# An attention and two MLPs in one kernel: new costs and due times for the planner that orders its instructions

## The chip, the cores and the metric

The kernel runs on one core of a Trainium2 chip. The metric is the device time of one execution in microseconds (us), taken as the median of three runs. The core has five engines that run their own instruction streams: TensorE (PE, matmuls and transposes; its weight loads are shown apart as PEld), VectorE (DVE), ScalarE (ACT), GpSimd (POOL) and SyncE (SP, here only DMA issues). Each stream is in order, so the order in which the program hands instructions to an engine decides what waits behind what.

## The reference

Three stages follow each other, all in fp32, on 12480 tokens of 128 channels. (In the inputs that are used here all weights but two are drawn eight times larger; this changes no shape.)

```python
def mab(q, kv):                        # attention, scale = 1/sqrt(128)
    s = scale * (q @ kv.T); s = s - s.max(-1)
    a = exp(s); a /= a.sum(-1) + 1e-9
    return a @ kv
h = mab(inducing, x)                   # 32 inducing points look at 12480 tokens
x = mab(x, h)                          # 12480 tokens look at 32 points
hid = x @ w_in                         # 128 -> 2048
x = (max(hid, 0) + alpha * min(hid, 0)) @ w_out          # 2048 -> 128
h = x @ w_in2                          # 128 -> 2048
P = a[0] + a[1]*h + a[2]*h**2 + a[3]*h**3
Q = 1 + |b[0]|*|h| + |b[1]|*h**2
out = (P / (Q + 1e-6)) @ w_out2        # 2048 -> 128
```

## The kernel before

A first part, written out by hand (the token list `START` and the code around it), loads x, computes the first attention, prepares the weights and runs the first MLP of the first 480 tokens. It ends about 97 us into the span. What follows is the steady part, in which the change lies.

The steady part goes over NC = 26 chunks of 480 tokens. The 2048 hidden channels are 16 slices of 128. A unit is two slices, so a chunk has NU = 8 units, u = 0 to 7, and there are 208 units k in all. Per chunk and slice, in the kernel's own names:

- First MLP. `la1` is a matmul (L773) into the one bank `h1`. `r` is the ReLU on ScalarE (L778) that empties that bank into SBUF; there are ten SBUF buffers. `lb` is the fp32 matmul back (L786, two records each in the trace) that adds into the one accumulator bank `acc`. After the 16th `lb` one more matmul (L788) adds the linear share, and `x2f` (ScalarE, L802) copies the bank out, `x2h` and `x2l` split the result into two parts.
- Second MLP. `l2` is three fast matmuls per slice (L827 to L829) into one of two double banks `h`. Then per unit: `s` (ScalarE square, L839), `A` (GpSimd, L848), `m` (VectorE, L860), `z` (ScalarE, L844), `q` (VectorE, L873, which frees the `h` bank), `rho` and `r0` (ScalarE, L877 and L882), `ee` and `r1` (VectorE, L892 and L896) and `g` (GpSimd, L907). For u = 7 the last steps are `g0` and `g` on VectorE (L902, L909). Per pair of units there is `B` (GpSimd, L853) and `P` (L864), a DMA issued from GpSimd's queue that adds the tile `b` onto the tile `m` in SBUF; `g` of both units needs it to have landed.
- `o` is the fp32 matmul out (L921, two records each) that adds `g` into the same bank `acc`; after 16 of them `oa` (ScalarE, L933) copies it out, `ot` transposes it on TensorE (L940, again through the bank `h1`), `oy` (L947) copies it and SyncE stores it.
- `at` (L614) transposes the attention weights of a later chunk through `h1` and `as_` (L619) copies them out.

So `acc` changes hands twice per chunk: from the `lb` of one chunk over `x2f` to the `o` of the chunk before, and back over `oa`. `h1` is shared by `la1`, `at` and `ot`.

The order of these instructions is not written by hand. `graph` builds a list of operations, each with its engine, a cost from `COST`, what it must come after, which bank it takes or gives back, and a due time: the unit's nominal start (k times TU = 5.376 us) plus an offset from `DUE`. `arranged` then plays this forward: on each engine it takes the operation that could start first, or one that could start up to `SLACK` later and has an earlier due time. A result is seen on another engine `LAG` after its end, and a bank comes back `LAG` after its reader's end. Only the resulting order goes to the chip. There the engines wait on semaphores, not on planned times.

Of the kernel before, what the change touches and what calls it, by code (L numbers as in the profile page):

```python
# [33 lines left out]


COST = dict(
    la1=0.22, lb=0.81, l2=0.65, o=0.81, mst=0.22, tr=0.51, r=0.46, cp=0.5, s=0.89, z=0.88, rho=0.92, r0=0.9,
    m=1.07, q=1.13, ee=1.07, g0=1.07, r1=1.07, g=1.07, A=1.11, B=2.1, P=0.9, gp=2.22, xl=1.22, cv=0.75,
    sm=(1.04, 0.71, 0.6, 0.55, 0.22), scl=0.45, hi=0.95, lo=2.5, landing=7.0, store=3.0,
)  # L40
LAG = 0.09
TU = 5.376
DUE = dict(
    x2f=3.01, la=1.34, span=1.32, lb1=-1.5, at=-14.51, l2=-9.14, s=-7.21, A=-10.84, m=-29.21, B=-5.93,
    P=-17.7, z=0.92, q=6.15, rho=10.6, r0=9.24, ee=14.43, r1=12.09, g0=15.76, g=14.81, gp=25.78, o=11.51,
    o1=-0.77, ot=6.24, pack=18.22,
)
# [6 lines left out]
def graph(NC, NU, due):  # L54


    ops = {}

    def add(name, eng, cost, after, t, late=0.0, take=None, give=None):
        ops[name] = eng, cost, late, [a for a in after if a in ops or a[0] in LATER], take, give, t  # L60

    C, NUN, CT = COST, NC * NU, NU * TU
    LATER = ("r",)
    add(("x2a", 0), "A", C["cp"], [], 0)
    add(("x2b", 0), "V", 0.66, [("x2a", 0)], 0)
    for i in range(4):
        add(("abs", i), "A", 0.45, [("cv", 4 * i - 8)], 0.5 + 1.2 * i)
        for n in range(max(4 * i - 3, 0), 4 * i + 1):
            add(("cv", n), "V", C["cv"], [("cv", n - 1), ("abs", (n - 1) // 4 if n else -1)], 1.2 * n)
    add(("conv",), "V", 0.0, [("cv", 12)], 1.2 * 13)  # L70
    add(("w2l", 3), "G", 1.25, [], 1)
    for c in range(NC):
        at = c * CT
        x2 = at - due["x2f"]
        if c > 1:
            g, half = c // 4, [("hi", c // 4, 1), ("lo", c // 4, 1)]
            t = x2 - CT - due["at"]
# [24 lines left out]
        for k in range(NU * c, NU * c + NU):
            t, j, odd, dve = k * TU, k // 2, k % 2, k % NU in DVE_G
            for i in range(2):
                add(
                    ("l2", k, i), "P", C["l2"],
                    [("x2l", c), ("x2b", c), ("w2l", 3), ("q", k - 2), ("l2", k, i - 1)], t + due["l2"] + 0.7 * i,
                )
            if c == NC - 1:
                add(("warm", k), "P", 0.5, [("l2", k, 1)], t + due["l2"] + 2.5, take="h1", give="h1")  # L110
            over = [] if odd else [("q", k - 4), ("q", k - 3), ("B", j - 2)]
            add(("s", k), "A", C["s"], [("l2", k, 1)] + over, t + due["s"])
            add(("A", k), "G", C["A"], [("s", k), ("m", k - 2)], t + due["A"])
            add(("m", k), "V", C["m"], [("A", k), ("o", 2 * (j - MBUFS) + 1, 1)], t + due["m"])
            if odd:
                add(("B", j), "G", C["B"], [("s", k), ("P", j - 2)], t + due["B"])
                add(("P", j), "G", C["P"], [("m", k), ("m", k - 1), ("B", j)], t + due["P"], late=C["landing"])
            add(("z", k), "A", C["z"], [("m", k)], t + due["z"])
            add(("q", k), "V", C["q"], [("z", k), ("conv",)] + ([("g", k - ZBUFS)] if k >= ZBUFS else []), t + due["q"])
            add(("rho", k), "A", C["rho"], [("q", k), ("r0", k - 2)], t + due["rho"])  # L120
            bank = [("g" if (k - 1) % NU in DVE_G else "r1", k - 1)]
            add(("r0", k), "A", C["r0"], [("rho", k)] + bank, t + due["r0"])
            add(("ee", k), "V", C["ee"], [("r0", k)], t + due["ee"])
            if dve:
                add(("g0", k), "V", C["g0"], [("ee", k)], t + due["g0"])
                add(("g", k), "V", C["g"], [("g0", k)], t + due["g"])
# [18 lines left out]
def arranged(NC, NU, due=None, span=False):  # L145
    ops = graph(NC, NU, due or DUE)
    names = list(ops)
    at = {n: i for i, n in enumerate(names)}
# [938 lines left out]
```

## Time and profile before

| | before |
|---|---|
| median of 3 runs | 1231.67 us (1231.12 to 1231.79) |
| the profiled execution, its own time | 1232.65 us |
| its span, first to last instruction | 1230.6 us |
| mean granted TensorE clock | 0.993 of full speed |
| busy PE / PEld / DVE / ACT / POOL | 96% / 55% / 84% / 88% / 83% |

The times are those of whole executions; the span lies inside the profiled execution's own time. Durations overlap: an instruction's interval in the trace includes the fill and drain of its pipeline, so the step from one start to the next on a busy engine is often shorter than the interval, and a busy TensorE is not one that loses nothing. On TensorE a sum is therefore made of steps between starts.

### The profile page before, as it was taken

How to read it: one execution, taken by the hardware profiler on the slowest of the kernel's cores; microseconds unless marked ns; L12 is line 12 of the kernel's file. 1: busy time of each engine (PE TensorE's matmuls, PEld its weight loads, DVE VectorE, ACT ScalarE, POOL GpSimd, SP SyncE). 2: the span in 40 equal slices, each digit the busy share in tenths (PEclk: the TensorE clock that was granted, in tenths of full speed). 3: DMA queues.
4: the chain of work that ended last, by engine and by line, in shares of the span. 5: the costliest groups of instructions: out<-in, count | busy, mean ns of one | idle time of the engine just before them, and what ended most of it. 6: DMA issues, size and time to landing. Idle time of an engine off the chain costs nothing.

```text
span 1230.6 us, 12439 instructions
## 1 busy us (share of the span) xinstructions
PE 1176.3 (96%) x4137; PEld 676.0 (55%) x4137; DVE 1032.0 (84%) x1006; ACT 1085.3 (88%) x1485; POOL 1015.6 (83%) x693
## 2 busy tenths in 40 slices
PE   7798999999999999999999999999999999999995
PEld 4444555555555555555555555555555555555552
DVE  3597988888888888888888988888888889888886
ACT  4478989999999999999999999899999999999974
POOL 0126989998899989899988999988999898889886
PEclk9899999999999999999999999999999999999999
DMA  9701454454345545444554544454455445445553
GB/s 231 237 17 32 97 105 99 100 107 93 80 100 105 105 84 117 96 82 95 104 104 89 113 100 88 85 109 100 96 105 104 81 89 112 96 97 105 104 103 74
DMA packets 25260, 124.23 MB, mean 101 GB/s; under 512 B 2428, under 2 KB 6812, under 8 KB 24684
## 3 DMA queue, kind: packets, MB, share of 16 engines
q0 software_dynamic: 14976, 102.24, 41.5%
q1 hardware_dynamic: 10220, 21.20, 6.3%
q8 instruction: 33, 0.54, 0.2%
q14 instruction: 31, 0.25, 0.1%
HBM read 14.80 MB, written 6.39 MB: 17 GB/s over the span
## 4 chain that ended last, share of the span: by engine, by line
PE 72%; POOL 8%; ACT 8%; DVE 6%; issue 4%; DMA 3%; SPq 0%; POOLq 0%; ACTq 0%
PE xa L786 22%; PE oa L921 20%; PE h L773 7%; PE h L827 7%; PE h L829 6%; PE h L828 6%; POOL m L907 3%; ACT h L844 2%; POOL a L848 2%; DMA xs<-in_x_dram 2%; ACT r L778 2%; DVE m L860 2%; POOL b L853 1%; ACT r L882 1%; PE to L940 1%
## 5 line engine op out<-in xcount | busy, mean ns | idle before, releaser
L907 POOL TENSOR_TENSOR m<-m,z 128x960 f32<-128x960 f32 x182 | 449.0, 2481 | 1.5 <-DMA m<-b 1.5
L921 PE MATMUL oa<-m,w2o 128*128 128x480 f32 x832 | 376.1, 572 | 14.3 <-POOL m L907 7.3
L786 PE MATMUL xa<-r,w 128*128 128x480 f32 x832 | 364.4, 568 | 2.6 <-ACT o L933 2.5
L848 POOL TENSOR_SCALAR a<-s,co 128x960 f32<-128x960 f32 x208 | 257.9, 1253 | 72.5 <-ACT s L839 71.9
L892 DVE SCALAR_TENSOR_TENSOR z<-z,r 128x960 f32<-128x960 f32 x208 | 239.2, 1150 | 75.1 <-ACT r L882 74.7
L873 DVE SCALAR_TENSOR_TENSOR z<-s,bab,h 128x960 f32<-128x960 f32 x208 | 251.4, 1211 | 41.9 <-ACT h L844 40.1
L778 ACT ACTIVATE r<-h 128x480 f32<-128x480 f32 x416 | 236.5, 569 | 49.9 <-PE h L773 47.9
L860 DVE TENSOR_TENSOR m<-h,a 128x960 f32<-128x960 f32 x208 | 238.8, 1154 | 28.5 <-POOL a L848 22.7
L921 PEld LDWEIGHTS oa<-m,w2o 128*128 128x128 f32 x832 | 156.2, 191 | 125.2 <-issue 103.3
L786 PEld LDWEIGHTS xa<-r,w 128*128 128x128 f32 x832 | 156.5, 190 | 123.2 <-issue 109.1
L839 ACT ACTIVATE s<-h 128x960 f32<-128x960 f32 x208 | 201.3, 970 | 21.5 <-PE h L829 19.8
L773 PE MATMUL h<-stk,wst 128*128 128x480 f32 x416 | 209.9, 505 | 9.6 <-ACT r L778 8.1
L896 DVE SCALAR_TENSOR_TENSOR z<-z,r 128x960 f32<-128x960 f32 x182 | 209.5, 1151 | 4.3
L877 ACT ACTIVATE rho<-z 128x960 f32<-128x960 f32 x208 | 209.5, 1007 | 2.3 <-DVE z L873 2.2
L853 POOL TENSOR_SCALAR b<-s,co 128x1920 f32<-128x1920 f32 x104 | 211.3, 2032 | 0.0
L882 ACT ACTIVATE r<-rho 128x960 f32<-128x960 f32 x208 | 202.6, 974 | 6.8 <-DVE z L896 5.7
L844 ACT ACTIVATE h<-h 128x960 f32<-128x960 f32 x208 | 200.1, 964 | 7.7 <-DVE m L860 4.1
L827 PE MATMUL h<-xh,w2h 128*128 128x480 f32 x416 | 183.4, 441 | 3.8 <-DVE z L873 3.0
L829 PE MATMUL h<-xl,w2h 128*128 128x480 f32 x416 | 157.9, 380 | 0.0
L828 PE MATMUL h<-xh,w2l 128*128 128x480 f32 x416 | 157.9, 379 | 0.0
L773 PEld LDWEIGHTS h<-stk,wst 128*128 128x128 f32 x416 | 78.0, 188 | 134.6 <-ACT r L778 114.0
L864 POOL DMA_DIRECT2D m<-b x104 | 92.4, 888 | 44.2 <-POOL b L853 26.8
(132 smaller groups left out, 787.5 us busy)
## 6 DMA issues: line engine op xcount, KB each, us to landing
m<-b POOLq DMA_DIRECT2D x104, 960.0 KB, 6.7
xs<-in_x_dram SPq DMA_DIRECT2D x13, 480.0 KB, 14.0
out_dram<-y SPq DMA_DIRECT2D x25, 240.0 KB, 4.2
raw<-in_moe_w_in_dram SPq DMA_DIRECT2D x4, 1024.0 KB, 5.3
raw<-in_moe_w_out_dram SPq DMA_DIRECT2D x4, 1024.0 KB, 12.8
out_dram<-y SPq DMA_DIRECT2D x2, 120.0 KB, 1.9
ind<-in_inducing_dram SPq DMA_DIRECT2D x1, 16.0 KB, 1.8
c<-in_moe_a_dram SPq DMA_DIRECT2D x1, 0.0 KB
```

What stands on the lines that cost most here:

```text
L773: nc.tensor.matmul(t[:, :W], lhsT=wst[:, f * P : (f + 1) * P], rhs=stk[c], start=True, stop=True)
L778: nc.scalar.activation(out=r, in_=h1s.pop((p, i))[:, :W], func=AF.Relu)
L786: nc.tensor.matmul(xacc[c][:, :W], lhsT=w1[:, f, :], rhs=rls.pop((p, i)), start=f == 0, stop=False)
L827: nc.tensor.matmul(t, lhsT=w2h[:, sl], rhs=xh, start=True, stop=False)
L828: nc.tensor.matmul(t, lhsT=w2l[:, sl], rhs=xh, start=False, stop=False)
L829: nc.tensor.matmul(t, lhsT=w2h[:, sl], rhs=xl, start=False, stop=True)
L848: nc.gpsimd.tensor_scalar(out=a, in0=S[k], scalar1=co[:, 3:4], scalar2=co[:, 1:2], op0=ALU.mult, op1=ALU.add)
L860: nc.vector.tensor_tensor(out=Mm[k], in0=hs_[k][:, :, :W], in1=A_.pop(k), op=ALU.mult)
L873: nc.vector.scalar_tensor_tensor(out=Z[k], in0=S.pop(k), scalar=bab[:, 1:2], in1=z, op0=ALU.mult, op1=ALU.add)
L892: nc.vector.scalar_tensor_tensor(out=Z[k], in0=Z[k], scalar=QC, in1=R0[k][:, :, :W], op0=ALU.add, op1=ALU.mult)
L907: nc.gpsimd.tensor_tensor(out=Mm[k], in0=Mm[k], in1=Z.pop(k), op=ALU.mult)
L921: nc.tensor.matmul(oacc[c][:, :W], lhsT=w2o[:, f, :], rhs=(G[k] if i == 0 else G.pop(k))[:, i], start=f == 0, stop=f == NF - 1)
```

## The change

No instruction is added or removed, and no tile, buffer or engine changes. What changes are the numbers with which the planner works, and a few of its rules:

- `COST`: most costs get a third digit and move by one to some per cent. The larger moves: `tr` (a group of four transposes) 0.51 to 0.42, `P` 0.9 to 0.66, `hi` 0.95 to 0.8, `xh` gets a cost of its own (0.57), a landing 7.0 to 6.5, a store 3.0 to 4.0.
- `LAG`: one value of 0.09 becomes one per engine: 0.2 after TensorE, 0.15 after ScalarE, 0.17 after VectorE, 0.14 after GpSimd.
- `STALL`: an operation on TensorE that starts later than the engine was free costs 0.1 more.
- `DUE`: new offsets, and for the steps of a unit eight values, one for each u, in place of one.
- `SLACK` goes from 0.18 to 0.1, and `EARLY` (a limit so wide that it never bound) goes.

```diff
 COST = dict(
-    la1=0.22, lb=0.81, l2=0.65, o=0.81, mst=0.22, tr=0.51, r=0.46, cp=0.5, s=0.89, z=0.88, rho=0.92, r0=0.9,
-    m=1.07, q=1.13, ee=1.07, g0=1.07, r1=1.07, g=1.07, A=1.11, B=2.1, P=0.9, gp=2.22, xl=1.22, cv=0.75,
-    sm=(1.04, 0.71, 0.6, 0.55, 0.22), scl=0.45, hi=0.95, lo=2.5, landing=7.0, store=3.0,
+    la1=0.217, lb=0.804, l2=0.651, o=0.804, mst=0.2, tr=0.42, r=0.455, cp=0.47, xh=0.57, s=0.865, z=0.855, rho=0.9,
+    r0=0.89, m=1.07, q=1.127, ee=1.072, g0=1.072, r1=1.072, g=1.072, A=1.118, B=2.15, P=0.66, gp=2.26, xl=1.174, cv=0.75,
+    sm=(1.04, 0.71, 0.6, 0.55, 0.22), scl=0.45, hi=0.8, lo=2.56, landing=6.5, store=4.0,
 )
-LAG = 0.09
+LAG = dict(P=0.2, A=0.15, V=0.17, G=0.14, S=0.0)
+STALL = 0.1
 DUE = dict(
-    x2f=3.01, la=1.34, span=1.32, lb1=-1.5, at=-14.51, l2=-9.14, s=-7.21, A=-10.84, m=-29.21, B=-5.93,
-    P=-17.7, z=0.92, q=6.15, rho=10.6, r0=9.24, ee=14.43, r1=12.09, g0=15.76, g=14.81, gp=25.78, o=11.51,
-    o1=-0.77, ot=6.24, pack=18.22,
+    x2f=-0.45, la=-9.06, span=2.97, lb1=-13.61, at=-97.53, o=-23.76, o1=-13.46, ot=22.31, pack=12.69,
+    l2=(29.67, 35.58, -79.83, -40.1, -11.09, -27.3, -24.5, -43.29),
+    s=(-17.84, -32.0, -16.83, -26.56, -59.46, -97.25, -31.04, -54.94),
+    A=(-63.73, -120.71, -103.15, -88.14, -48.47, -71.46, -128.35, -89.09),
...
+    B=(-54.95, -120.41, -105.91, -26.76, 36.86, -21.45, -83.45, 36.32),
+    P=(187.3, 56.68, 20.63, 25.06, 67.81, -5.11, 38.88, -25.19),
...
+    gp=(89.99, 44.35, 54.18, 117.38, 95.33, 178.76, 75.12, 95.23),
 )
-EARLY, SLACK = 9007.5, 0.18
+SLACK = 0.1
...
-            add(("x2h", c), "A", C["cp"], [("x2f", c), ("l2", NU * (c - 2) + NU - 1, 1)], x2 + 0.6)
+            add(("x2h", c), "A", C["xh"], [("x2f", c), ("l2", NU * (c - 2) + NU - 1, 1)], x2 + 0.6)
...
-            t, j, odd, dve = k * TU, k // 2, k % 2, k % NU in DVE_G
+            t, j, odd, u = k * TU, k // 2, k % 2, k % NU
...
-            add(("s", k), "A", C["s"], [("l2", k, 1)] + over, t + due["s"])
+            add(("s", k), "A", C["s"], [("l2", k, 1)] + over, t + due["s"][u])
...
-                s = max(free[e], ready[i], bank[take[i]], when[i] - EARLY)
+                s = max(free[e], ready[i], bank[take[i]])
...
-        free[e] = t = s + cost[i]
+        free[e] = t = s + cost[i] + (STALL if e == "P" and s > free[e] + 1e-9 else 0.0)
...
-            bank[give[i]] = t + LAG
+            bank[give[i]] = t + LAG[e]
...
-            ready[n] = max(ready[n], t + late[i] + (LAG if eng[n] != e or late[i] else 0.0))
+            ready[n] = max(ready[n], t + late[i] + (LAG[e] if eng[n] != e or late[i] else 0.0))
```

The other steps of a unit (`m`, `z`, `q`, `rho`, `r0`, `ee`, `g0`, `g`, `r1`) get their eight values and their `[u]` in the same way. P and B exist for odd u alone.

## Rows read from the trace of the kernel before

**Rows 1.** the page, costliest groups: us busy, mean ns of one

```profile
L786 PE MATMUL xa<-r,w 128*128 128x480 f32 x832 | 364.4, 568 | 2.6 <-ACT o L933 2.5
```

**Rows 2.** table by stretch: length; busy PE, PEld, DVE, ACT, POOL; clock; DMA; GB/s

```profile
96.80:132.38 35.58, 29.59 (x87) 15.80 (x86) 27.28 (x31) 30.16 (x43) 23.71 (x19) 0.95 0.27 55
132.38:183.71 51.33, 47.73 (x152) 27.25 (x150) 46.40 (x43) 46.91 (x63) 46.20 (x30) 0.97 0.50 102
656.61:699.34 42.73, 42.36 (x139) 24.40 (x138) 37.02 (x34) 39.69 (x54) 36.98 (x25) 1.00 0.48 99
699.34:742.74 43.40, 42.52 (x139) 24.38 (x138) 37.21 (x36) 40.66 (x56) 39.43 (x28) 1.00 0.47 97
183.71:1171.24 987.53, 976.73 (x3153) 560.41 (x3152) 853.52 (x772) 918.95 (x1232) 882.49 (x596) 1.00 0.48 98
1171.24:1230.60 59.36, 45.39 (x139) 25.05 (x137) 46.47 (x43) 36.62 (x42) 44.85 (x29) 0.96 0.45 92
```

**Rows 3.** timeline of TensorE, two stretches (start, us, engine, line)

```profile
609.30 4.99 PE L786 MATMUL xa<-r,w 128*128 128x480 f32 x12
...
656.61 0.75 PE L788 MATMUL xa<-stk,mst 128*128 128x480 f32 x1
657.20 0.57 PE L614 MATMUL ta<-ident,a 120*128 120x120 f32 x4
658.06 2.65 PE L921 MATMUL oa<-m,w2o 128*128 128x480 f32 x6 [0.28 <-issue]
...
661.59 0.49 PE L773 MATMUL h<-stk,wst 128*128 128x480 f32 x1
661.92 0.38 PE L827 MATMUL h<-xh,w2h 128*128 128x480 f32 x1
...
662.35 0.38 PE L829 MATMUL h<-xl,w2h 128*128 128x480 f32 x1
662.74 0.49 PE L773 MATMUL h<-stk,wst 128*128 128x480 f32 x1
...
664.36 0.38 PE L773 MATMUL h<-stk,wst 128*128 128x480 f32 x1
...
667.08 0.49 PE L773 MATMUL h<-stk,wst 128*128 128x480 f32 x1
...
668.23 0.49 PE L773 MATMUL h<-stk,wst 128*128 128x480 f32 x1
...
669.58 0.48 PE L773 MATMUL h<-stk,wst 128*128 128x480 f32 x1
```

**Rows 4.** timeline of ScalarE in the same stretch

```profile
662.12 0.57 ACT L778 ACTIVATE r<-h 128x480 f32<-128x480 f32 x1 [0.58 <-PE h L773]
662.59 0.97 ACT L882 ACTIVATE r<-rho 128x960 f32<-128x960 f32 x1
```

**Rows 5.** waits of the weight loads, 183.71 to 1171.24 us: total, times, longest

```profile
PEld h L773 <- ACT r L778: 93.9, 183, 0.8
...
PEld h L827 <- DVE z L873: 9.7, 33, 0.4
```

**Rows 6.** timeline of TensorE where the accumulator changes hands the other way

```profile
721.13 0.75 PE L773 MATMUL h<-stk,wst 128*128 128x480 f32 x1
722.41 1.07 PE L786 MATMUL xa<-r,w 128*128 128x480 f32 x2 [0.53 <-ACT o L933]
```

**Rows 7.** timeline of GpSimd at the end of a chunk

```profile
654.62 2.16 POOL L853 TENSOR_SCALAR b<-s,co 128x1920 f32<-128x1920 f32 x1
657.09 0.88 POOL L864 DMA_DIRECT2D m<-b  x1 [0.30 <-POOL b L853]
...
665.05 1.14 POOL L848 TENSOR_SCALAR a<-s,co 128x960 f32<-128x960 f32 x1 [1.45 <-ACT s L839]
```

**Rows 8.** timeline of VectorE, first reader of that DMA's result

```profile
664.66 1.16 DVE L902 TENSOR_TENSOR r<-m,r 128x960 f32<-128x960 f32 x1
```

**Rows 9.** the page, DMA issues (KB each, us from issue to landing)

```profile
m<-b POOLq DMA_DIRECT2D x104, 960.0 KB, 6.7
```

More of the change, by code (lines that the diff above doesn't have):

```diff
@@ L36 @@
 COST = dict(
-    la1=0.22, lb=0.81, l2=0.65, o=0.81, mst=0.22, tr=0.51, r=0.46, cp=0.5, s=0.89, z=0.88, rho=0.92, r0=0.9,
-    m=1.07, q=1.13, ee=1.07, g0=1.07, r1=1.07, g=1.07, A=1.11, B=2.1, P=0.9, gp=2.22, xl=1.22, cv=0.75,
-    sm=(1.04, 0.71, 0.6, 0.55, 0.22), scl=0.45, hi=0.95, lo=2.5, landing=7.0, store=3.0,
-)
-LAG = 0.09
+    la1=0.217, lb=0.804, l2=0.651, o=0.804, mst=0.2, tr=0.42, r=0.455, cp=0.47, xh=0.57, s=0.865, z=0.855, rho=0.9,
+    r0=0.89, m=1.07, q=1.127, ee=1.072, g0=1.072, r1=1.072, g=1.072, A=1.118, B=2.15, P=0.66, gp=2.26, xl=1.174, cv=0.75,
+    sm=(1.04, 0.71, 0.6, 0.55, 0.22), scl=0.45, hi=0.8, lo=2.56, landing=6.5, store=4.0,
+)
+LAG = dict(P=0.2, A=0.15, V=0.17, G=0.14, S=0.0)
+STALL = 0.1
 TU = 5.376
 DUE = dict(
-    x2f=3.01, la=1.34, span=1.32, lb1=-1.5, at=-14.51, l2=-9.14, s=-7.21, A=-10.84, m=-29.21, B=-5.93,
-    P=-17.7, z=0.92, q=6.15, rho=10.6, r0=9.24, ee=14.43, r1=12.09, g0=15.76, g=14.81, gp=25.78, o=11.51,
-    o1=-0.77, ot=6.24, pack=18.22,
+    x2f=-0.45, la=-9.06, span=2.97, lb1=-13.61, at=-97.53, o=-23.76, o1=-13.46, ot=22.31, pack=12.69,
+    l2=(29.67, 35.58, -79.83, -40.1, -11.09, -27.3, -24.5, -43.29),
+    s=(-17.84, -32.0, -16.83, -26.56, -59.46, -97.25, -31.04, -54.94),
+    A=(-63.73, -120.71, -103.15, -88.14, -48.47, -71.46, -128.35, -89.09),
+    m=(-108.75, -22.15, -116.09, -46.72, -47.13, -42.75, -50.15, -148.19),
+    B=(-54.95, -120.41, -105.91, -26.76, 36.86, -21.45, -83.45, 36.32),
+    P=(187.3, 56.68, 20.63, 25.06, 67.81, -5.11, 38.88, -25.19),
+    z=(-26.7, -63.52, -31.2, -26.94, 5.39, 24.47, 11.89, 15.71),
+    q=(32.02, 39.1, 47.63, 65.87, 13.6, 133.96, 50.31, 70.75),
+    rho=(36.83, 86.45, 150.83, 117.66, 71.04, 81.94, 112.77, 38.48),
+    r0=(78.33, 29.52, 26.2, -49.91, 50.51, 19.63, -30.96, -28.81),
+    ee=(62.9, 108.52, 89.98, 43.06, 77.86, 74.23, 43.3, 78.62),
+    g0=(70.57, 75.02, 1.99, 84.61, 105.19, 73.56, 80.62, 149.83),
+    g=(58.94, 3.2, 116.11, 8.69, 83.04, 10.67, 31.27, 107.91),
+    r1=(40.2, 67.74, 21.19, 94.45, -8.56, 116.72, 111.67, -32.38),
+    gp=(89.99, 44.35, 54.18, 117.38, 95.33, 178.76, 75.12, 95.23),
 )
-EARLY, SLACK = 9007.5, 0.18
+SLACK = 0.1
 DVE_G = (7,)
@@ L106, in graph @@
                     ("l2", k, i), "P", C["l2"],
-                    [("x2l", c), ("x2b", c), ("w2l", 3), ("q", k - 2), ("l2", k, i - 1)], t + due["l2"] + 0.7 * i,
+                    [("x2l", c), ("x2b", c), ("w2l", 3), ("q", k - 2), ("l2", k, i - 1)], t + due["l2"][u] + 0.7 * i,
                 )
             if c == NC - 1:
-                add(("warm", k), "P", 0.5, [("l2", k, 1)], t + due["l2"] + 2.5, take="h1", give="h1")
+                add(("warm", k), "P", 0.5, [("l2", k, 1)], t + due["l2"][u] + 2.5, take="h1", give="h1")
@@ L111, in graph @@
             over = [] if odd else [("q", k - 4), ("q", k - 3), ("B", j - 2)]
-            add(("s", k), "A", C["s"], [("l2", k, 1)] + over, t + due["s"])
-            add(("A", k), "G", C["A"], [("s", k), ("m", k - 2)], t + due["A"])
-            add(("m", k), "V", C["m"], [("A", k), ("o", 2 * (j - MBUFS) + 1, 1)], t + due["m"])
+            add(("s", k), "A", C["s"], [("l2", k, 1)] + over, t + due["s"][u])
+            add(("A", k), "G", C["A"], [("s", k), ("m", k - 2)], t + due["A"][u])
+            add(("m", k), "V", C["m"], [("A", k), ("o", 2 * (j - MBUFS) + 1, 1)], t + due["m"][u])
@@ L115, in graph @@
             if odd:
[L116 to L120, printed above, removed]
-            bank = [("g" if (k - 1) % NU in DVE_G else "r1", k - 1)]
@@ L122, in graph @@
[L122 to L126, printed above, removed]
-            else:
-                add(("r1", k), "V", C["r1"], [("ee", k)], t + due["r1"])
-                add(("g", k), "G", C["gp"], [("r1", k)], t + due["gp"])
+                add(("B", j), "G", C["B"], [("s", k), ("P", j - 2)], t + due["B"][u])
@@ new lines, in graph @@
+                add(("P", j), "G", C["P"], [("m", k), ("m", k - 1), ("B", j)], t + due["P"][u], late=C["landing"])
+            add(("z", k), "A", C["z"], [("m", k)], t + due["z"][u])
+            add(("q", k), "V", C["q"], [("z", k), ("conv",)] + ([("g", k - ZBUFS)] if k >= ZBUFS else []), t + due["q"][u])
+            add(("rho", k), "A", C["rho"], [("q", k), ("r0", k - 2)], t + due["rho"][u])
+            bank = [("g" if (k - 1) % NU in DVE_G else "r1", k - 1)]
+            add(("r0", k), "A", C["r0"], [("rho", k)] + bank, t + due["r0"][u])
@@ L130, in graph @@
+            add(("ee", k), "V", C["ee"], [("r0", k)], t + due["ee"][u])
+            if u in DVE_G:
+                add(("g0", k), "V", C["g0"], [("ee", k)], t + due["g0"][u])
+                add(("g", k), "V", C["g"], [("g0", k)], t + due["g"][u])
+            else:
+                add(("r1", k), "V", C["r1"], [("ee", k)], t + due["r1"][u])
+                add(("g", k), "G", C["gp"], [("r1", k)], t + due["gp"][u])
             if odd:
-                for u in (k - 1, k):
-                    ops["g0" if ("g0", u) in ops else "g", u][3].append(("P", j))
+                for n in (k - 1, k):
+                    ops["g0" if ("g0", n) in ops else "g", n][3].append(("P", j))
```

## The prediction, made before the change was run

> **What bounds the kernel now.** I read the table by stretch first. The steady part, 183.71 to 1171.24 us, is 23 chunks and takes 987.53 us, 42.94 us a chunk; single chunks take 42.73 to 43.40 [rows 2]. TensorE shows 976.73 us busy there. That looks full, but its intervals overlap, so I counted the work of a chunk by steps between starts. The step inside a run of `lb` or `o` records is 0.402 us: twelve records last 4.99, of which the last alone is 0.568, and 4.42 / 11 = 0.402 [rows 1, 3]. The step of an `l2` matmul is 0.217: 661.92 to 662.35 is two steps, 0.43 [rows 3]. A `la1` into which the engine flows takes the same step. A chunk has 64 records of 0.402 (25.73), 48 `l2` steps, 16 `la1` and one closing matmul (65 x 0.217 = 14.11), and eight transposes of about 0.10 (0.84): 40.7 us. So TensorE loses 42.94 - 40.7 = 2.2 us a chunk, 52 us in the steady part. ScalarE with 918.95 / 23 = 39.95 and GpSimd with 38.4 us busy a chunk lie just under it [rows 2]. TensorE is the bound, with little room beneath it.
>
> Then the timeline of TensorE at the start of a chunk, for where the 2.2 us go [rows 3]. The reader is to see two kinds of hole.
>
> First, `la1`. The one at 664.36 has an interval of 0.38; those at 661.59, 662.74, 667.08, 668.23 and 669.58 have 0.48 or 0.49, about 0.11 more: their weight load waited for the ReLU to empty the bank `h1`. With one slice of `l2` between two of them, 661.59 to 662.74 is 1.15 where 0.217 + 0.651 = 0.868 is work: 0.28 lost. With one `o` between, 667.08 to 668.23 is 1.15 against 0.217 + 0.804 = 1.02: 0.13. The next, 1.35, loses 0.33. With 0.11 for the first and for the one at 667.08 that is 0.96 us in this chunk. Over 23 chunks: 6.4 us behind one `l2` slice and 15.7 behind one `o` or `lb`. The chain of waits over the stretch agrees in kind: 183 weight loads of `la1`, eight a chunk, waited for the ReLU, whereas only 33 of `l2` waited for `q` [rows 5].
>
> Second, the accumulator. From the transposes at 657.20 (0.42 of work) to the first `o` at 658.06 there are 0.44 us lost while `x2f` empties `acc` [rows 3]; 23 times, 10.1 us. On the way back, at 722.41, `lb` finds TensorE idle for 0.53 us [rows 6]; I saw it in the chunks of 43.40 us, at most every fourth, about 3 us in all.
>
> Outside the steady part TensorE is idle for 35.58 - 29.59 and 51.33 - 47.73, together 9.6 us, in the first two chunks and 59.36 - 45.39 = 14.0 us in the last stretch [rows 2].
>
> **The change, part by part.** No instruction is added or taken away, so every gain and loss is a wait that the new order has or lacks.
>
> *The bank `h1`.* Under the old numbers a `la1` is thought to be possible 0.09 + 0.46 + 0.09 = 0.64 after the last, which fits behind one `l2` slice (0.65). The new ones say 0.2 + 0.455 + 0.15 = 0.805. The trace sides with the new: a ReLU behind which ScalarE flows on takes 0.47 from start to start [rows 4], and behind one slice 0.28 is lost. With 0.805 the bank is 0.154 late behind a slice, more than the new `SLACK` of 0.1, so the planner puts something else there. I take all 6.4 us of that. Behind one `o` or `lb` (0.804) it is late by 0.001, within `SLACK`, and `la1` is due earlier than most of those, so the rule of choice still takes it and pays `STALL`; only where the offsets arrange it otherwise does the hole go. I take 4 of 15.7 us; the ends are 0 and 15.7.
>
> About this hole the Trainium skill has a rule: TensorE's queue can pull a weight load ahead of matmuls in flight (page "TensorE: Matmul & The Clock Gate", section "Architectural detail: the array is 16× 32×32, not 1× 128×128"). By it the 0.11 would be hidden and only the 0.154 would be worth anything; the trace disagrees for a load that itself waits for a semaphore, which shows 0.11 more each time [rows 3].
>
> *The accumulator.* The old numbers see 0.09 + 0.5 + 0.09 against 0.51 of transposes, 0.17 of waiting; the new 0.2 + 0.47 + 0.15 - 0.42 = 0.40. What could fill it is `l2`, if it is not yet done, or a second transpose, which shares `h1`. I expect little: 1 of 10.1 us, ends 0 and 10.1. On the way back 1 of 3, ends 0 and 3.
>
> *First chunks and tail.* 23.6 us of idle time, set by the latency through four engines. The offsets differ by u only and not by chunk, so they are not made for these ends. I take a gain of 3, with -5 and +8 as ends.
>
> *P and GpSimd.* Before, `P` is due 17.7 before its unit, ahead of `A` (10.84 before). Now `P` of u = 7 is due 25.19 before its unit, but `A` of the next unit 63.73 - 5.38 = 58.35 before that same point: whenever both are ready, `A` goes first (1.12 by its new cost, 1.14 in the trace [rows 7]), and in places a `B` with it, whose step to the next start is 657.09 - 654.62 = 2.47 [rows 7]. `P` then goes out up to 3.6 us later. It lands 6.7 us after its issue [rows 9]; the one of 657.09 is first read at 664.66, 7.57 later, so the cover is 0.87 us [rows 7, 8]. Beyond it `g0` waits on VectorE, with the `m` of the next unit queued behind it, and `g` waits on GpSimd with the next `A` behind it. I take a loss of 3 us over the run, with 0 and 20 as ends (rival D).
>
> *Sum.* 6.4 + 4 + 1 + 1 + 3 - 3 = 12.4 us. The profiled execution's own time is 1232.65, which gives 1220.3; the median lies 0.98 below that execution, so 1219.3: **1219 us**.
>
> **Rivals.**
>
> A, *smaller gain: the held weight load is no loss*. If TensorE would have spent the 0.11 anyway, only 0.154 x 23 = 3.5 of the `la1` holes can go: 3.5 + 0 + 1 + 1 + 3 - 3 = 5.5, 1226 us. For it: the skill's rule above. Against it: the steps of 1.15 in [rows 3].
>
> B, *larger gain*. All 22 us at `h1`, half of the 10.1 at `acc` and 1 on the way back, with no loss on GpSimd: 28, so 1203.6 us. For it: the new numbers see these holes at nearly their measured size. Against it: the choice is greedy, and at `acc` little is at hand.
>
> C, *no change*. TensorE's holes close and the time appears as waits for `g` or `q`, because the loop through ScalarE, GpSimd and VectorE sets the pace, or because the order comes out nearly the same: 1231.7 us. For it: ScalarE at 39.95 of 42.94. Against it: 33 waits for `q` of 9.7 us in 23 chunks [rows 5], and ScalarE's steps are shorter than its intervals (0.47 for 0.57 [rows 4]).
>
> D, *slower, through `P` on GpSimd*. If `P` of u = 7 goes behind one `A` and one `B` in each chunk, it is 3.6 - 0.87 = 2.7 us late. GpSimd idles 42.94 - 38.4 = 4.5 us a chunk [rows 2] and takes up part; if 0.8 us a chunk is left over, 25 chunks lose 20 us. The gains of the sum, 15.4, come to half at most while TensorE waits for `g`: 20 - 7.7 = 12 us slower, 1244 us. It decides as soon as `P` of units 6 and 7 stands more than 0.87 us later against its first reader, so that DMA waits of `g` and `g0` appear in every chunk. For it: the cover is short and the due times allow it. Against it: the planner makes `g` wait for a landing of 6.5, so it can see this loss.
>
> **How the numbers follow.** A measurement of this kernel can tell about 0.2% (2.5 us) from no change. The forecast has 0.52, with its own range 1206 to 1229, from the ends of its terms; A 0.08; B 0.12; C 0.10; D 0.18. Faster is forecast, A and B: 0.72. Same is C: 0.10. Slower is D: 0.18. The range goes down to B's 1203 and up to 1240, which leaves half of B and over half of D out, 0.16.
>
> **What would show it.** Right: in the steady part fewer than the 183 waits of `la1` for the ReLU, none behind a single `l2` slice, a chunk of 42.2 to 42.6 us, and the hole before the first `o` still there. Wrong: the same count of waits with a shorter chunk (then the gain lies elsewhere), waits of `g` and `g0` for the DMA in each chunk (D), more waits of `l2` for `q` (C), or a change that lies in the first 184 or last 60 us.

## The result and the profile after

The changed kernel takes 1215.89 us in the median of four runs (1215.13 to 1218.17), the kernel before 1231.73 us in four runs on the same chip. The ratio is 0.9875 with a 95% interval of 0.9858 to 0.9892: 15.8 us less, and the interval lies clear of 1. The profiled execution has a span of 1214.3 us, 16.3 less than before.

The table by stretch of the changed kernel, with the columns of [rows 2] and cut at the same events (where the `lb` chains of chunks 0, 1, 2 and 25 end, with their closing matmul; the two single chunks in the middle are rows 3 and 4):

```profile
95.85:131.22 35.37, 30.03 (x88) 16.57 (x86) 25.46 (x29) 28.41 (x41) 22.12 (x18) 0.90 0.28 56
131.22:182.15 50.93, 45.60 (x151) 26.65 (x150) 45.82 (x43) 46.77 (x62) 47.20 (x32) 1.00 0.50 102
646.95:688.45 41.50, 41.10 (x139) 24.83 (x138) 36.97 (x35) 39.09 (x54) 37.17 (x25) 1.00 0.50 101
688.45:732.05 43.60, 42.00 (x140) 24.81 (x138) 37.49 (x36) 39.77 (x56) 39.90 (x27) 1.00 0.48 96
182.15:1152.71 970.56, 953.94 (x3153) 569.82 (x3152) 857.51 (x773) 907.71 (x1232) 883.62 (x596) 1.00 0.49 100
1152.71:1214.30 61.59, 47.72 (x139) 25.91 (x137) 48.91 (x46) 38.56 (x45) 46.26 (x29) 0.92 0.43 88
```

The reader is to see where the time went. The steady part of 23 chunks fell from 987.53 to 970.56 us, by 17.0, or 0.74 a chunk. The two first chunks together fell by 0.6 us, the last stretch grew by 2.2. And the chunks are less alike than before: they come in a cycle of four, and the last two of it take about 41.5 us (before: about 42.8), the second 42.2 (before: 42.9), the first 43.60 (before: 43.40).

The timeline of TensorE at the start of a good chunk, against [rows 3] (`la1` is L787, `l2` L841 to L843, `o` L935, the closing matmul L802, `at` L628):

```profile
646.95 0.76 PE L802 MATMUL xa<-stk,mst 128*128 128x480 f32 x1
647.54 0.57 PE L628 MATMUL ta<-ident,a 120*128 120x120 f32 x4
648.52 2.65 PE L935 MATMUL oa<-m,w2o 128*128 128x480 f32 x6 [0.40 <-POOL b L867]
...
651.88 0.38 PE L841 MATMUL h<-xh,w2h 128*128 128x480 f32 x1
...
652.53 0.38 PE L787 MATMUL h<-stk,wst 128*128 128x480 f32 x1
652.75 0.38 PE L841 MATMUL h<-xh,w2h 128*128 128x480 f32 x1
...
658.15 0.75 PE L787 MATMUL h<-stk,wst 128*128 128x480 f32 x1
658.74 1.77 PE L935 MATMUL oa<-m,w2o 128*128 128x480 f32 x4
...
661.64 0.38 PE L787 MATMUL h<-stk,wst 128*128 128x480 f32 x1
...
663.17 0.38 PE L787 MATMUL h<-stk,wst 128*128 128x480 f32 x1
663.39 1.77 PE L935 MATMUL oa<-m,w2o 128*128 128x480 f32 x4
664.88 0.50 PE L787 MATMUL h<-stk,wst 128*128 128x480 f32 x1
```

The reader is to see two things. First, between one `la1` and the next there are now mostly two `o` (four records), two `lb`, two slices of `l2`, or a mix of them; those at 652.53, 661.64 and 663.17 have the interval 0.38 of one that TensorE flows into. The ones at 658.15 and 664.88 show 0.75 and 0.50, but they begin while the `o` before them still stream (663.39 + 4 x 0.402 = 665.00) and lose nothing: the interval alone does not tell, the step does. Second, the hole at the accumulator is still there, 0.40 us idle before 648.52, longer than the 0.28 of before. The view puts it down to `b` on GpSimd, which ended last; the `g` that this `o` reads were done long before, and what it waits for is `x2f`, which empties the bank just then:

```profile
647.85 0.57 ACT L816 COPY xf<-xa 128x480 f32<-128x480 f32 x1
```

To have the whole steady part and not one chunk, I went over all TensorE records of it and added up by how much each ends later than its work (0.402 or 0.217 us, the steps of the prediction) after the end of the one before it. The sums, sorted by what came too late, in us over the 23 chunks:

| kernel | `la1` held | `l2` late | first `o` or `lb` after `acc` changes hands, and other late `o`, `lb` | steady part |
|---|---|---|---|---|
| before | 23.1 | 10.0 | 15.8 | 987.5 |
| after | 8.5 | 7.1 | 17.6 | 970.6 |
| e1_old_offsets | 13.8 | 10.6 | 28.5 | 991.8 |
| e2_old_numbers | 33.2 | 16.5 | 26.0 | 1014.9 |
| e3_la1_earlier | 64.9 | 2.8 | 18.0 | 1024.7 |
| e4_h1_later | 4.5 | 33.1 | 27.1 | 1001.9 |
| s_old | 24.6 | 7.7 | 15.8 | 987.2 |
| s_new | 11.9 | 10.5 | 26.3 | 986.5 |
| s_lag | 14.4 | 10.3 | 22.2 | 985.4 |
| s_cst | 29.9 | 11.3 | 18.7 | 997.4 |
| s_fix | 6.3 | 2.3 | 15.3 | 962.8 |
| e7_no_scale | 4.0 | 4.4 | 17.7 | 963.5 |

From before to after 14.6 us go at `la1` and 2.9 at `l2`; small waits before `ot`, which the table leaves out, give 0.9, and the accumulator costs 1.8 more. That is 16.6 of the 17.0 us.

### The profile page after: what moved, and what is told of

Same layout as the page of the kernel before. It is cut to its first block, busy times and chain, and to the rows that moved or that the text cites. A ratio compares the mean times of both kernels' runs of the same rounds, so it can differ in the third digit from the quotient of the medians.

```text
span 1214.3 us, 12431 instructions
## 1 busy us (share of the span) xinstructions
PE 1154.3 (95%) x4137; PEld 686.4 (57%) x4137; DVE 1035.9 (85%) x1006; ACT 1074.2 (88%) x1485; POOL 1017.5 (84%) x693
## 3 DMA queue, kind: packets, MB, share of 16 engines
q0 software_dynamic: 14976, 102.24, 42.2%
## 4 chain that ended last, share of the span: by engine, by line
PE 60%; POOL 15%; DVE 10%; ACT 8%; issue 3%; DMA 3%; SPq 0%; POOLq 0%; ACTq 0%
PE oa L935 19%; PE xa L800 16%; POOL m L921 6%; PE h L787 6%; PE h L841 5%; PE h L843 5%; PE h L842 5%; POOL a L862 4%; POOL b L867 4%; DVE m L874 3%; DMA xs<-in_x_dram 2%; DVE z L887 2%; ACT s L853 2%; DVE z L906 2%; ACT r L896 2%
## 5 line engine op out<-in xcount | busy, mean ns | idle before, releaser
L921 POOL TENSOR_TENSOR m<-m,z 128x960 f32<-128x960 f32 x182 | 430.3, 2463 | 36.8 <-DVE z L910 35.4
L935 PE MATMUL oa<-m,w2o 128*128 128x480 f32 x832 | 373.2, 572 | 16.1 <-POOL b L867 7.6
L800 PE MATMUL xa<-r,w 128*128 128x480 f32 x832 | 376.1, 570 | 3.3 <-ACT o L947 2.8
L862 POOL TENSOR_SCALAR a<-s,co 128x960 f32<-128x960 f32 x208 | 248.8, 1217 | 36.8 <-ACT s L853 34.9
L874 DVE TENSOR_TENSOR m<-h,a 128x960 f32<-128x960 f32 x208 | 235.8, 1154 | 39.5 <-POOL a L862 38.9
L887 DVE SCALAR_TENSOR_TENSOR z<-s,bab,h 128x960 f32<-128x960 f32 x208 | 247.2, 1209 | 2.3 <-ACT h L858 1.5
L787 PE MATMUL h<-stk,wst 128*128 128x480 f32 x416 | 236.8, 570 | 10.5 <-ACT r L792 10.4
L935 PEld LDWEIGHTS oa<-m,w2o 128*128 128x128 f32 x832 | 156.1, 191 | 140.0 <-issue 109.7
L800 PEld LDWEIGHTS xa<-r,w 128*128 128x128 f32 x832 | 155.3, 190 | 107.3 <-issue 87.8
L853 ACT ACTIVATE s<-h 128x960 f32<-128x960 f32 x208 | 197.0, 971 | 20.8 <-PE h L843 18.4
L858 ACT ACTIVATE h<-h 128x960 f32<-128x960 f32 x208 | 199.6, 964 | 13.6 <-DVE m L874 11.8
L867 POOL TENSOR_SCALAR b<-s,co 128x1920 f32<-128x1920 f32 x104 | 205.4, 1975 | 0.0
L841 PE MATMUL h<-xh,w2h 128*128 128x480 f32 x416 | 186.9, 449 | 6.6 <-DVE z L887 6.2
L843 PE MATMUL h<-xl,w2h 128*128 128x480 f32 x416 | 157.9, 379 | 0.0
L787 PEld LDWEIGHTS h<-stk,wst 128*128 128x128 f32 x416 | 78.4, 189 | 115.6 <-ACT r L792 92.9
L878 POOL DMA_DIRECT2D m<-b x104 | 92.4, 888 | 33.2 <-POOL b L867 30.6
## 6 DMA issues: line engine op xcount, KB each, us to landing
xs<-in_x_dram SPq DMA_DIRECT2D x13, 480.0 KB, 13.9
raw<-in_moe_w_out_dram SPq DMA_DIRECT2D x4, 1024.0 KB, 11.9
```

Source lines behind the costliest of these rows:

```text
L787: nc.tensor.matmul(t[:, :W], lhsT=wst[:, f * P : (f + 1) * P], rhs=stk[c], start=True, stop=True)
L800: nc.tensor.matmul(xacc[c][:, :W], lhsT=w1[:, f, :], rhs=rls.pop((p, i)), start=f == 0, stop=False)
L841: nc.tensor.matmul(t, lhsT=w2h[:, sl], rhs=xh, start=True, stop=False)
L862: nc.gpsimd.tensor_scalar(out=a, in0=S[k], scalar1=co[:, 3:4], scalar2=co[:, 1:2], op0=ALU.mult, op1=ALU.add)
L867: nc.gpsimd.tensor_scalar(out=b, in0=SP.pop(j), scalar1=co[:, 2:3], scalar2=co[:, 0:1], op0=ALU.mult, op1=ALU.add)
L874: nc.vector.tensor_tensor(out=Mm[k], in0=hs_[k][:, :, :W], in1=A_.pop(k), op=ALU.mult)
```

## The experiments

A word on what the theories of the later runs rest on. The planner's play-forward can also be used the other way: keep an order as it is and play it with other numbers. With the changed kernel's numbers the order of the kernel before ends 21.1 us after that of the changed kernel, though its own plan, made with the old numbers, ended 5.0 us before the changed kernel's. These are ends on paper, and no times of the chip; only their differences are used, and the runs are the test of them. (Code cuts below are shortened.)

**Half of the change at a time.** e1 has the new numbers and the old offsets:

```diff
 COST, LAG, STALL, SLACK: as changed
-    l2=(29.67, 35.58, -79.83, ...), s=(-17.84, ...), ...
+    x2f=3.01, la=1.34, ..., l2=-9.14, s=-7.21, ...        # as before, the same for every u
```

> The changed kernel's costs, lags, stall and slack with the single offsets of the kernel before. In this order 47 la1 stand behind one o, 14 behind one lb and none behind one l2 slice (before: 84, 19 and 25). Theory T (the gain is TensorE no longer held at the bank h1, whatever offsets bring it about): 42 x 0.13 + 25 x 0.28 = 12.5 us less than before, about 1219. Rival R (the gain comes from the eight offsets per step, the new numbers by themselves do nothing): about 1231.

Measured: 1239.15 us, ratio 1.006 (1.004 to 1.0081). Both theories miss. The holds of `la1` did fall, from 23.1 to 13.8 us, but the first `o` and `lb` on a changed accumulator lost 28.5 in place of 15.8.

e2 is the other half:

```diff
 DUE: as changed
-COST = dict(la1=0.217, ...); LAG = dict(P=0.2, A=0.15, V=0.17, G=0.14, S=0.0); STALL = 0.1; SLACK = 0.1
+COST = dict(la1=0.22, ...);  LAG = dict.fromkeys("PAVGS", 0.09);               STALL = 0.0; SLACK = 0.18
+            over = [("s", k - 1)] if odd else [...]       # and m after the m of its pair
```

> The kernel before's costs, lag, slack and no stall with the changed kernel's eight offsets per step (and two added precedences that keep the halves of a pair in order). In this order 101 la1 stand behind one o, 27 behind one lb, 26 behind one l2 slice. Theory T: those holds cost as before, 1231 or more (before had 128 of them, this has 154: up to 1235). Rival R: the offsets alone bring the gain, about 1216 to 1220.

Measured: 1266.8 us, ratio 1.0281 (1.026 to 1.0302). Rival R falls: the eight offsets by themselves bring no gain, they lose 34.8 us. Theory T has the direction, but only 10 of the 27 us more in the steady part are holds of `la1`; the rest is `l2` and the accumulator. So each half alone is slower than before, and the two together are faster.

**The holds of `la1` alone.** e3 moves only `la1`, only on TensorE:

```diff
+        if run[n][0] == "la1" and run[n - 2][0] == run[n - 1][0] in ("o", "lb") and run[n - 3][0] == "la1":
+            run[n - 1], run[n] = run[n], run[n - 1]
```

> The changed kernel with the order of TensorE alone altered: 109 more la1 stand behind one o or lb, each moved ahead of one of the two that it stood behind; all other engines keep their order. Theory T: 109 x 0.12 = 13 us more than the changed kernel, about 1229. Rival A of the prediction (a held weight load is no loss, or TensorE makes it up): no change, 1216.

Measured: 1271.12 us, ratio 1.0323 (1.0298 to 1.0347), 55 us more than the changed kernel. A held `la1` is a loss, so the rival of this run falls, but the price was far off: 56.4 us more of holds, 0.5 us for each of the 109 and not 0.12. The timeline says why. TensorE and then ScalarE, at one such place (`la1` is L800, `lb` L813, `s` L866, `r` L805):

```profile
701.60 0.38 PE L800 MATMUL h<-stk,wst 128*128 128x480 f32 x1
701.82 0.96 PE L813 MATMUL xa<-r,w 128*128 128x480 f32 x2
703.28 0.48 PE L800 MATMUL h<-stk,wst 128*128 128x480 f32 x1 [0.50 <-ACT r L805]
```

```profile
701.80 0.97 ACT L866 ACTIVATE s<-h 128x960 f32<-128x960 f32 x1
702.67 0.56 ACT L805 ACTIVATE r<-h 128x480 f32<-128x480 f32 x1
```

The `la1` of 701.60 is done soon, but ScalarE's next instruction in its order is `s`, and `r` comes after it, at 702.67. So the bank is free only at 703.2, and TensorE stood idle 0.50 us. In the steady part 127 `la1` now stand behind one `o` or `lb`, and lose 64.9 us. 69 of them have `s` in front of their `r` in this way, and lose 53 us; 40 lose the 0.12 that was expected. An order is one thing over all engines, and a move on one of them alone meets the places of the others.

e4 gives the old planner one better number:

```diff
-            bank[give[i]] = t + LAG
+            bank[give[i]] = t + LAG + (0.35 if give[i] == "h1" else 0.0)
```

> The kernel before with one number altered: the planner counts the bank h1 as free 0.35 us later than it did (0.99 us after la1 in place of 0.64). In this order 18 la1 stand behind one o, 14 behind one lb, none behind one l2 slice. Theory T: 66 x 0.13 + 5 x 0.13 + 25 x 0.28 = 16 us less than before, about 1216. Rival R: the old offsets keep the old pace, about 1231.

Measured: 1247.8 us, ratio 1.0129 (1.0104 to 1.0154). The holds fell to 4.5 us, more than in the changed kernel, and the time rose all the same: `l2` was late by 33.1 us in place of 10.0. In the list of waits its weight loads wait longer for `q`, the reader that frees their bank (before, 9.7 us in 33 [rows 5]):

```profile
PEld h L827 <- DVE z L873: 24.5, 38, 1.2
```

This is rival C's mechanism, the loop over `q`, in a kernel whose order was not made for it, and the accumulator cost 11.3 us more besides. Theory T in its simple form (remove the holds and the time follows) is thereby out. What the chip pays is all waits together.

**Is it the numbers or the freedom of the offsets?** That is theory F against rival S, as the two expectations below put them. For s_old and s_new I searched offsets for each u anew, with the same start, the same random steps and the same count, once with the old numbers and once with the new:

```diff
 s_old:  COST, LAG = 0.09, no STALL, SLACK = 0.18 as before;  DUE searched (8 per step)
 s_new:  COST, LAG per engine, STALL, SLACK = 0.1 as changed;  DUE searched (8 per step)
 both, and s_lag, s_cst, s_fix below: s and m of a pair in order, as in e2
```

(With the changed kernel's own offsets this addition leaves the order as it is.)

> Offsets for each u, searched anew by 400,000 random steps that shorten the planner's own end, with the kernel before's costs, lag and slack and no stall, starting from the single offsets of the kernel before. Its plan ends 0.8 us before the plan of the kernel before and 13.6 us before that of s_new. Theory F (the chip follows the new numbers, so a plan made with the old ones slips): played forward with the new numbers this order ends 1.0 us later than before's, so about 1232, and later than s_new. Rival S (the freedom of eight offsets and the search make the gain): clearly faster than before, 1216 to 1225, and if the old plan held, faster than s_new.

Measured: 1234.2 us, ratio 1.0008 (0.9995 to 1.0021). As theory F says: a plan that is shorter on paper than before's is not faster on the chip.

> The same search, the same start and the same number of steps, but with the changed kernel's costs, lags, stall and slack. Theory F: its plan ends 13.2 us before the order of the kernel before played with the same numbers, and 7.8 us after the changed kernel's, so about 1218 to 1224. Rival S: no faster than s_old.

Measured: 1229.61 us, ratio 0.9972 (0.9961 to 0.9984). Faster than s_old by 4.6 us, with a plan that is 13.6 us longer: rival S is not borne out. The size is missed: 1218 to 1224 was expected. The holds of `la1` halved, but the accumulator cost 26.3 us. My search also ended 7.8 us short of the changed kernel's offsets on paper; on the chip it is 13.7.

Then each half of the new numbers with the same search:

```diff
 s_lag:  LAG per engine as changed;  COST, SLACK, no STALL as before;  DUE searched
 s_cst:  COST, STALL, SLACK as changed;  LAG = 0.09 as before;  DUE searched
```

> As s_old, but of the changed kernel's numbers the planner has the lags alone (0.2, 0.15, 0.17, 0.14 in place of 0.09); costs, slack and the missing stall are the kernel before's; the same search, start and number of steps. Theory L (of the new numbers the lags carry the gain): played with all new numbers this order ends 9.9 us before s_old's, so 1222 to 1230, faster than before. Rival (costs and stall carry it): as s_old, 1232 or more.

> The other half: the changed kernel's costs, stall and slack with the old lag of 0.09 on every engine; the same search. Theory L: its plan promises a pace that the chip does not hold; played with all new numbers it ends 4.7 us after s_old's, so 1235 to 1242. Rival: the costs and the stall are enough, 1216 to 1228.

Measured: s_lag 1228.52 us, ratio 0.9976 (0.9961 to 0.9991); s_cst 1238.8 us, ratio 1.0051 (1.0031 to 1.007). In these searches it is the lags that matter. In the orders made with 0.09 (e4 with its extra 0.35 aside) `la1` is held 23 to 33 us on the chip, in those made with the new lags 6 to 14 (e3, which was altered afterwards, aside). But each set of numbers was searched once. The changed kernel's offsets, with the same numbers as s_new, are 13.7 us faster than s_new, so what a search happens to find weighs more than the 5 to 10 us between these four runs. That the lags carry the gain is supported by them and not shown.

**`P` on GpSimd (rival D).** e5 moves `P` of units 6 and 7 in the kernel before, e6 every `P` in the changed one, in both behind the next operation of GpSimd:

```diff
+        if ops[n][0] == "P":                         # e5: only u = 6, 7; not where the next one is a g that reads it
+            ops.insert(next_of_pool(n), ops.pop(n))
```

> The kernel before with the 26 P of units 6 and 7 moved behind the next operation of GpSimd (a g, 2.2 us); all other orders unchanged. Their cover before the first reader was 0.8 to 1.5 us, so they land about 1.3 us too late. Theory D of the prediction (a P that loses its cover sets the pace): 0.8 to 1.35 us a chunk, 20 to 34 us more, 1252 to 1266. Rival: GpSimd's and VectorE's idle time takes it up, 1232 to 1236.

Measured: 1236.41 us, ratio 1.0032 (1.0017 to 1.0047). The wait is there, in the list of waits of this run (24 times, `g0` for the DMA; before, 1.0 us in 3):

```profile
DVE r L913 <- DMA m<-b: 18.1, 24, 1.9
```

But the steady part grew by 1.5 us only, the last stretch by 3.7. The rest of the waits cost nothing on TensorE in the steady part. The price of D, 0.8 us a chunk, was about twelve times too high for the 0.75 us that a landing was late here on average; 2.7 us, as D had it, was not tried.

> The changed kernel with all 104 P moved behind the next operation of GpSimd (mostly a g of 2.2 us or x2l of 1.2). In its trace a P starts 10.0 to 13.9 us before its first reader, 3.3 us or more beyond the landing of 6.7. If only the cover counts: 1216, no change. If a later P costs by itself (the DMA's traffic meets other work, or g behind it comes too early and holds GpSimd): 1220 or more.

Measured: 1230.3 us, 14.4 more than the changed kernel, so the first bound falls. The steady part lost 4.4 us, the first two chunks 6.8 and the last stretch 2.9. GpSimd's waits for the DMA, 1.5 us or less in either kernel, came to 2.7 us in the steady part, 5.9 before it and 4.8 behind it: the covers that I read were those of the steady part, and at the ends, where nothing fills TensorE, they were shorter. How much of the 4.4 us is landing and how much the changed order of `g` I did not separate.

**All waits together.** No single wait gave the times of these runs, but the play-forward has them. With the changed kernel's numbers the orders of e1, e2, e3, e4 and e6 end 20.8, 53.7, 59.4, 37.5 and 13.3 us after the changed kernel's, and those of s_old, s_new, s_lag and s_cst 22.1, 7.8, 12.2 and 26.8; measured were 23.3, 50.9, 55.2, 31.9 and 14.4, and 18.3, 13.7, 12.6 and 22.9. Only e5 is far off, 17.0 us over the kernel before where 4 to 5 were measured, and there the landing is the reason: `P` with 0.66, 6.5 and a lag of 0.14 lands 7.3 us after its start in the plan and 6.7 in the trace [rows 9], and with a landing of 5.9 the play-forward gives 4.4.

**Where the changed plan slips.** I set the planner's own start of each operation against the start in the trace. In the kernel before the operations fall behind their plan by 1.3 us over one chunk (`g` at 657.73 by 0.0, `g` at 703.87 by 1.3), a little at every hold. In the changed kernel it is 0.3 us over a chunk, until one place in every fourth chunk. GpSimd there (`g` L921, the scaling of the attention weights L595, `A` L862):

```profile
692.08 2.52 POOL L921 TENSOR_TENSOR m<-m,z 128x960 f32<-128x960 f32 x1
695.02 1.05 POOL L595 TENSOR_TENSOR att<-att,mm 120x512 f32<-120x512 f32 x1 [0.41 <-DVE mm L594]
696.03 2.23 POOL L921 TENSOR_TENSOR m<-m,z 128x960 f32<-128x960 f32 x1
698.25 1.14 POOL L862 TENSOR_SCALAR a<-s,co 128x960 f32<-128x960 f32 x1
```

The scaling waits 0.41 us for two VectorE instructions that the planner doesn't know, and takes 1.0 us to the next start where `COST` says 0.45. The `g` at 696.03 and what follows it on GpSimd are 1.2 to 1.4 us further behind the plan than what came before. e7 leaves the scaling out:

```diff
     def a_scale(g):
-        ...; nc.vector.tensor_scalar(...); nc.vector.reciprocal(...); nc.gpsimd.tensor_tensor(...)
+        SUM.pop(g)
```

> The changed kernel in its own order, without the scaling of the attention weights of the later chunks (two VectorE instructions and one on GpSimd, six times; the weights stay unnormalised). In the changed kernel's trace the operations behind it start 1.2 to 1.4 us later than planned from there on. Theory F: the six chunks of 43.6 us lose about 1.3 us each, 8 us in all, 1208. Rival: those chunks are long because of the hi and lo parts, 1215 to 1217.

Measured: 1207.82 us, ratio 0.9798 (0.9779 to 0.9817), 8 us less, and the chunk in question in the table by stretch:

```profile
516.39:558.73 42.34, 41.48 (x140) 24.89 (x138) 36.51 (x34) 39.55 (x56) 38.87 (x26) 1.00 0.49 99
```

42.34 us against 43.60. The other three kinds of chunk are as they were. That is the time that theory F gave. The hi and lo parts, which e7 still has, are not what these 1.3 us were; but e7 takes away work as well as a wrong number, and does not tell the two apart.

s_fix does the full work and tells the planner of it:

```diff
-    ..., scl=0.45, hi=0.8, lo=2.56, landing=6.5, store=4.0,
+    ..., scd=0.47, scl=1.03, hi=0.68, lo=1.45, landing=6.5, store=4.0,
...
-                add(("scl", g), "G", C["scl"] * n, [("sm", g, 4), ("at", c - 1)], tg - 2)
+                add(("scd", g), "V", C["scd"], [("sm", g, 4), ("scl", g - 1)], tg - 3)
+                add(("scl", g), "G", C["scl"] * n, [("scd", g), ("at", c - 1)], tg - 2)
...
+ DUE: searched again from the changed kernel's offsets
```

> The changed kernel's numbers with four of them set to what its trace shows: the scaling of the attention weights (scl) 1.03 in place of 0.45 with its two VectorE instructions as an operation of their own (0.47), lo 1.45 in place of 2.56, hi 0.68 in place of 0.8; then the same search from the changed kernel's offsets. Theory F: played with these numbers its plan ends 12.4 us before the changed kernel's order, so about 1204. Rival: what is left is latency that no number holds, 1213 to 1219.

Measured: 1206.44 us, ratio 0.9789 (0.9769 to 0.9808). It is faster than both kernels, by 9.5 us than the changed one, where 12 were expected. Its steady part in the table by stretch, and the chunk that was 43.60:

```profile
180.06:1142.84 962.78, 952.09 (x3153) 568.47 (x3152) 853.68 (x770) 904.96 (x1231) 880.82 (x596) 1.00 0.49 101
682.62:724.13 41.51, 41.08 (x139) 24.91 (x138) 37.18 (x35) 40.23 (x57) 40.16 (x28) 1.00 0.44 89
```

41.86 us a chunk, 1.2 above the counted work of 40.7, and over half of that is the accumulator. The gain lies where the changed plan slipped: of the cycle of four chunks the first is 2.1 us shorter, and the others, but for three single ones, are within 0.2 us of what they were. What the four numbers did is not separated on the chip, one from the other or from the further search. On paper the scaling is the smaller part: with `scl` put back and `scd` taken out the changed kernel's order ends 4.6 us earlier and this one at the same point, whereas with `lo` put back to 2.56 this one ends 11.1 us later.

## Why the prediction was right

The forecast was 1219 us, 12.4 us of gain; measured were 15.8, within its own range of 1206 to 1229. That range is not what the ends of the terms add up to (18.6 us slower to 43.2 faster), so to land in it took some luck: the mechanism at `la1` was right, and the errors of the other terms nearly cancelled. By its steps:

- *What bounds the kernel.* TensorE, with 2.2 us lost a chunk: right. The losses that went are TensorE's, and in this change the time followed them.
- *`la1` behind one `l2` slice*, 6.4 us: right. After the change no `la1` of the steady part stands there; with the new lags its bank would be late by 0.154, more than `SLACK`.
- *`la1` behind one `o` or `lb`*, 4 of 15.7: mis-sized. About 8 went in the balance (14.6 of 23.1 in all, less the 6.4). Of the loss behind one `o` or `lb` itself nearly all went: 96 `la1` stood there in the steady part and lost 15.8 us, 22 stand there now and lose 3.1. The other `la1` lose 5 us where they lost 1, 3.5 of it in five of the chunks in which the plan slips. I held that the rule of choice would still take a bank that is late by 0.001. It would, but the offsets arrange it otherwise: two units go through their `l2` together, and two `o` stand between `la1`. The witness that I named failed as well: 186 loads wait for the ReLU, where 183 did. By my own list the same count with a shorter chunk was to mean that the gain lies elsewhere; it does not, and it was the sign that was badly chosen. The chunk of 42.2 to 42.6 us came out at 42.20 on average, with single ones from 41.5 to 43.6.

The list of waits of the weight loads in the changed kernel, against [rows 5]:

```profile
PEld h L787 <- ACT r L792: 76.9, 186, 1.5
...
PEld h L841 <- DVE z L887: 4.9, 23, 0.2
```

The count of waits is the same and the time only 17 us less, because a load may wait while the matmuls before it still stream, as at 664.88 above. What costs is the step beyond the work, and that is what has to be counted.

- *The accumulator*, 1 + 1 us of gain: wrong in sign, a loss of 1.8. It is the way to `o` that lost; the way back costs the same 4 us as before. That nothing is at hand to fill it was right; the new order has `at` there as before.
- *First chunks and tail*, a gain of 3: the chunks gained 0.6, the tail lost 2.2, and the hand-ordered part ahead of them came out 0.9 shorter: 0.7 lost in sum, inside the ends that I gave. The idle time of TensorE, which the term was about, grew from 23.6 to 24.5 us over the three stretches. In the last one it is 13.9 us as before (14.0), and what grew is the busy time, 47.72 for 45.39 with the same 139 records: the granted clock was 0.92 there in place of 0.96. Around a wait of 5.03 us the table by stretch of TensorE alone (busy, clock, DMA, GB/s) goes from the full clock of 2.4 GHz to the lower level of 1.2, and eight `o` records take 5.70 us, where twelve `lb` took 4.99 at full clock [rows 3]:

```profile
1193.80:1197.20 3.40, 0.76 (x2) 1.00 0.00 0
1200.60:1204.10 3.50, 3.50 (x6) 0.50 0.52 105
```

```profile
1199.59 5.70 PE L935 MATMUL oa<-m,w2o 128*128 128x480 f32 x8 [5.03 <-POOL m L921]
```

- *`P`*, a loss of 3: none is seen. GpSimd around the `P` of units 6 and 7, against [rows 7]:

```profile
648.76 0.88 POOL L878 DMA_DIRECT2D m<-b  x1 [0.30 <-POOL b L867]
649.40 1.49 POOL L827 TENSOR_TENSOR xl<-xf,xh 128x480 fp32r<-128x480 f32 x1
...
660.42 2.55 POOL L921 TENSOR_TENSOR m<-m,z 128x960 f32<-128x960 f32 x1
```

`P` at 648.76 is now first read by the `g` at 660.42, 11.66 us later and not 7.57: the order gives more cover, not less. And e5 shows that landing 0.75 us late in each chunk would have cost 4 us and not 20.
- *`l2` late*, not a term of the sum: 2.9 us of gain.

The terms that I set too low (4 at `la1`, 3 at `l2`, 3 at `P`, and 1 of small waits before `ot`) against those set too high (4 at the accumulator, 4 at the ends) leave 3 us more gain, which is the 15.8 against 12.4. Rival A is out: behind one `o` or `lb`, where it gave nothing, 12.7 us went. And a held load is not free where the bank is hardly late: the 17 `la1` that still stand behind one `lb` lose 0.12 us each. One of them, 0.32 us from its start to the next where its work is 0.217; the ReLU that it waits for, which ends at 678.18; its weight load, at 678.23; and the load of the `la1` of 661.64, which began 0.21 us ahead of it:

```profile
677.41 0.97 PE L800 MATMUL xa<-r,w 128*128 128x480 f32 x2
678.23 0.48 PE L787 MATMUL h<-stk,wst 128*128 128x480 f32 x1
678.55 1.37 PE L800 MATMUL xa<-r,w 128*128 128x480 f32 x3
```

```profile
677.61 0.57 ACT L792 ACTIVATE r<-h 128x480 f32<-128x480 f32 x1 [0.23 <-PE h L787]
```

```profile
678.23 0.19 PEld L787 LDWEIGHTS h<-stk,wst 128*128 128x128 f32 x1 [0.63 <-ACT r L792]
...
661.43 0.19 PEld L787 LDWEIGHTS h<-stk,wst 128*128 128x128 f32 x1
```

The rule of the Trainium skill that stood beside it (page "TensorE: Matmul & The Clock Gate", section "Architectural detail: the array is 16× 32×32, not 1× 128×128") lets TensorE pull a weight load ahead of matmuls in flight. The section says nothing of a load whose semaphore is not yet up; these rows show one that waited, at 678.23, and it was not hidden; the load of 661.43, which did not wait, was. Rival C did not come (23 waits of `l2` for `q`, where there were 33), but e4 shows that its mechanism is real.

What stays open: why the orders of s_new and e1 let the first `lb` wait so long for `oa`, which costs them 12 and 11 us and the changed kernel 4 (the rest of their 26 to 28 us lies before the first `o`, as the changed kernel's 14 does); how e6's 4.4 us divide; and which of its numbers, or its search, made s_fix faster.

## What to carry to other kernels

Where a program orders its own instructions by a cost model, the hand-off times between engines deserve as much care as the durations: here an order made with lags of 0.09 in place of 0.14 to 0.2 us, and with the other old numbers, looked 5 us shorter and ran 16 us longer. Before an order is run, or one wait in it is given a price, play the whole of it forward with the best numbers: that came within 6 us of every altered order but e5's. Set each planned start against the trace; the first operation that falls behind points at a number that is wrong, and correcting four that the trace showed, with a new search, was worth 9.5 us more. New numbers need new priorities and the other way round: each half of this change was slower alone.

## What was not expected of the hardware

The order, played forward with a fixed number for each kind of operation and four lags, stayed within 0.4 us of the chip on all four engines through a whole chunk of 41.5 us. A DMA that landed 0.75 us too late on average, 24 times (18.1 us of waits), cost 1.5 us in the steady part. And a `la1` moved forward by one `o` or `lb` of 0.804 us cost 0.5 us on average, mostly because ScalarE, in its order, had another instruction ahead of its reader.
